# An adaLN block with sliding-window attention: V made per query group, an input load moved ahead, and packed matmul sums that choose their order

## The chip, the cores and the metric

The kernel runs on one core of a Trainium2 chip. The metric is the device time of one execution in microseconds (us), as the median of several runs. A core has a matmul engine (TensorE, PE), a vector engine (VectorE, DVE), an activation engine (ScalarE, ACT), a general engine (GpSimd, POOL) and a queue engine (SyncE, SP). They run in parallel, each in its own order, and wait for each other on semaphores. DMAs are issued from the queues of SP, ACT and POOL and share 16 DMA engines. The working memory SBUF has 128 rows, called partitions; matmuls write to PSUM, which has eight banks.

## What is computed

A transformer block over 2048 tokens of width 448, all in bf16, with six modulation rows made from a conditioning vector c. The attention has 16 heads of 28; each query sees 8 keys, at distances 0, 2, ..., 14 behind it.

```python
mod = (silu(c) @ w_mod).reshape(6, 448)            # sa, ca, ga, sb, cb, gb
h = layernorm(x) * (1 + ca) + sa
q, k, v = split(h @ wqkv)                          # 16 heads of 28
idx = pos[:, None] - 2 * arange(8)                 # keys of a query; masked where < 0
o = softmax(q . k[idx] * 28 ** -0.5) @ v[idx]
x = x + ga * (o @ wo)
h = layernorm(x) * (1 + cb) + sb
y = layernorm(h)                                   # the MLP has its own layernorm
x = x + gb * (gelu(y @ w1 + b1) @ w2 + b2)         # w1: 448 x 1792
```

## The kernel before

**Tokens.** The input is read so that even tokens make the first 1024 columns and odd tokens the second: with that order the dilated window of 8 becomes 8 neighbours. There are 16 blocks of 128 tokens, in four chunks of four blocks. Blocks 0 to 7 are the even tokens, 8 to 15 the odd ones.

**Front** (`front_ln`, `front_qk`). For each block VectorE takes statistics (L528, L529) and writes z, the normalized block (L551). For chunks 0 and 1 PE transposes z (L664) and VectorE and ACT write the modulated transpose hT (L679, L683); the factors come from PE matmuls on the first modulation load wm_st (L583). For chunks 2 and 3 the reciprocal root is taken on POOL (L546), SP issues one transposing DMA for each block (L688), and VectorE modulates in place (L692). Then Q and K are made, transposed, as four packed tasks for each group of blocks, and copied out by ACT (L732). V is made for two blocks of tokens at a time, tokens on partitions (pv, L609 and L615), and ACT copies it to vstage (L746). From there an ACT-queue DMA writes it to a DRAM buffer v_hbm (L750).

**Packed tasks** (`packed`). A width of 448 is 3.5 times 128. Two outputs are made together: three full matmuls of 128 rows each (`full`, L609) and one of 64 rows each (`half`, L615), the two of 64 rows in two halves of the array at once. Full and half are different array modes. Whether a task begins with full or with half is fixed by a turn counter of its kind (qk, v, w1), even or odd, so that two tasks of a kind in a row meet in the same mode.

**Attention** (`attention`). Queries are taken in 18 groups of 114, in 9 pairs b = 0 to 8. A group consists of two subgroups of 57 queries with 64 keys each. The logits of both subgroups of a group go to upper and lower partitions of a bank (lt, L829); ACT takes exponentials (et, L839), VectorE masks them (L847), PE makes denominators and outputs (pd L861, po L869), ACT inverts the denominators by logarithm and exponential (L882, L885), and VectorE multiplies (L895). The po matmuls need V in key rows: partitions 0 to 63 hold the keys of subgroup 0, and 64 to 127 those of subgroup 1, which begin 57 keys later. That is what the two SP-queue loads `vb<-v_hbm` of each pair (L815) bring.

**Behind it.** `out_proj` for each block: pw (L910), residual (L914), second layernorm, modulation (L925, L927), third layernorm to y, and a transposing DMA to yT (L936). `mlp` for each chunk: first layer p (L609, L615; seven packed tasks), gelu on ACT (L969), second layer (L982), residual (L990) and store. wo is scaled by ga (L776) and w2 by gb (L791) ahead of use. ga, sb, g2 and gb come from the later modulation: PE makes the rows from the loads wmod2 (L764), ACT evacuates them (L770) and writes them to DRAM (L772), and SP reads them back broadcast as mod_bc (L773).

**What sets the order.** Every instruction is a task with an engine, an assumed duration and buffers. `Planner.plan` tries 300 random perturbations of the priorities in a small timing model, keeps the cheapest plan, and `emit` writes each engine's instructions in that order. The seed fixes the draw. A task whose mode equals PE's current mode gets a bonus (SAME), a change of mode costs SWITCH in the model. ROOM holds the numbers of buffers. Bulk loads go on the POOL queue one after another (`bulk_loads`): wmod2 (4), wo (4), x of blocks 8 to 11, x of blocks 12 to 15, b2, w1 (4), w2 (4); each is released by a VectorE memset of one element (L385). The phases are: attention 0 to 4 and MLP 0, attention 5 and 6 and MLP 1, attention 7 and 8 and MLP 2 and 3.

Of the kernel before, what the change touches and what calls it, by code (L numbers as in the profile page):

```python
# [26 lines left out]
WQ, WK, WE = 57, 64, 58  # L27
SBQ, NSB, NBT = 2 * WQ, 18, 9
# [8 lines left out]
SEED, TURNS = 7, 300  # L37
QKE = ("AAAAAAAA", "AAAAAAAA")
# [6 lines left out]
FRONTS = (0, 1, 3)  # L45
LMM, DMM = 0.59, 1.0
FILL_UNTIL, FILL_SHARE = 12.0, 1.0
ROOM = {"S": 8, "et": 2, "den": 2, "zh": 6, "zb": 5, "T": 4, "hm": 4, "vb": 2, "vs": 2, "xp": 6}
DMA_RATE, TR_BYTES = 340e3, 400e3
SWITCH, SAME = 0.095, 1.0  # L50
SEM = 0.07
# [17 lines left out]
class Task:  # L69
    def __init__(self, n, eng, us, fn, bufs, rank_add, late, dense, port, mode):  # L70
        self.n, self.eng, self.us, self.fn, self.bufs = n, eng, us, fn, bufs
        self.name = f"{eng} {fn.__qualname__.split('.')[-1]}:{fn.__code__.co_firstlineno}"
        self.rank_add, self.late, self.dense, self.port = rank_add, late, dense, port
        self.mode_in, self.mode_out = mode if isinstance(mode, tuple) else (mode, mode)
        self.before, self.after = {}, []
        self.rank = 0.0
        self.fill = 0


class Planner:  # L80
# [68 lines left out]
    def forward(self):  # L149
# [13 lines left out]
        while len(order) < len(self.tasks):  # L163
            started = False
            for e in ("PE", "DVE", "ACT", "POOL", "SP", "BW"):
# [4 lines left out]
                for t in ready[e]:  # L170
                    if ready_at[t] > now or (shared and t.port):
                        continue
                    key = (-ready_at[t], -t.n) if e == 'BW' else (t.rank + (SAME if e == "PE" and t.mode_in == mode else 0.0), -t.n)
# [23 lines left out]
                if e == "PE" and t.mode_in != mode:  # L197
                    end += SWITCH
                    mode = t.mode_out
# [44 lines left out]
    def plan(self):  # L244
# [4 lines left out]
        for turn in range(TURNS):  # L249
# [4 lines left out]
            for again in range(3):  # L254
# [7 lines left out]
                if cost < best[2]:  # L262
                    best = ([(t, t.fill) for t in order], {b: b.slot for t in order for b in t.bufs}, cost)
                    starts = {t: t.start for t in order}
                    kept = used
# [7 lines left out]
    def emit(self):  # L273
        for t, fill in self.order:
            if fill:
                self.filler(fill)
            t.fn()
# [3 lines left out]
def kernel(  # L281
# [44 lines left out]
    v_hbm = hbm.tile([WT, DP], BF16, name="v_hbm")  # L326
# [28 lines left out]
    vstage = [cst.tile([128, 2, H, HP], BF16, name=f"vstage{i}") for i in range(ROOM["vs"])]  # L355
# [74 lines left out]
    def v_pads():  # L430
        z = warm_w[0:LEAD, :]
        o = v_hbm[0:LEAD, :]
        nc.sync.dma_start(out=bass.AP(o.tensor, o.offset, [[DP, LEAD], [(SL + SEP) * DP, 3], [1, DP]]),
                          in_=z.unsqueeze(1).to_broadcast([LEAD, 3, DP]))

    dma("SP", 0.5, v_pads, 3 * LEAD * DP * 2, ["v_pads"], reads=["warm_w"], order_after=chain["head"])
# [14 lines left out]
    def bulk_loads():  # L451
        for i in range(2):
            load_m(bulk, nc.gpsimd, lambda i=i: wmod2[i].t[:], (2 + 2 * i) * D, f"wmod2{i}", [wmod2[i]], True)
        wo_v = A_wo.rearrange("(ft r d) n -> r d ft n", r=4, d=DH)
# [3 lines left out]
        load_x(bulk, nc.gpsimd, 8, 12, True)  # L458
        load_x(bulk, nc.gpsimd, 12, 16, True)
# [49 lines left out]
    def consts():  # L509
        for vs in vstage:  # L510
            nc.gpsimd.memset(vs[:, :, :, DH:HP], 0.0)
# [89 lines left out]
    def packed(outs, w, x, turn):  # L601
# [3 lines left out]
        def full(last):  # L605
            for i in range(2):
                kts = (0, 3, 1 + i)
                for n, kt in enumerate(kts):
                    nc.tensor.matmul(outs[i].t[:], lhsT=w(i, kt, slice(0, 128)), rhs=x(i, kt, slice(0, 128)),  # L609
                                     start=(n == 0 and not last), stop=(n == 2 and last))  # L610

        def half(last):
            for i, kt, r0 in halves:
                rows = slice(r0, r0 + 64)
                nc.tensor.matmul(outs[i].t[:], lhsT=w(i, kt, rows), rhs=x(i, kt, rows),  # L615
                                 start=not last, stop=last, tile_position=(r0, 0))

        if turn % 2 == 0:
            full(False)
            half(True)  # L620
        else:
            half(False)
            full(True)

    def pack_mode(turn):
        return ("F", "64x128") if turn % 2 == 0 else ("64x128", "F")

    def pack_us(n):
        return 7 * (n / 2400 + 0.0025) + 0.008 + SWITCH

    turns = {"qk": 0, "v": 0, "w1": 0}
    h_of = {}

    def front_ln(bs):
        ch = bs[0] // 4
        early = ch <= 1
        if ch not in h_of:
            h_of[ch] = sb("T", [128, KT, 512], BF16, "hT")
# [12 lines left out]
        n, o = 128 * len(bs), (bs[0] % 4) * 128  # L651
# [35 lines left out]
        for b in bs:  # L687
            dma("SP", 1.25, lambda b=b: nc.sync.dma_start_transpose(out=hc.t[:, :, b % 4 * 128:b % 4 * 128 + 128], in_=zs[b].t[:]),  # L688
# [20 lines left out]
    def front_qk(bs, engs):  # L709
        n, c0, o = 128 * len(bs), tok_col(bs[0]), bs[0] % 4 * 128  # L710
        hc = h_of[bs[0] // 4]
        hk = [(hc, kt, b) for kt in range(KT) for b in bs]
        for mp in range(4):
            ms = (2 * mp, 2 * mp + 1)
            half = mp // 2
            pq = [ps_one([128, n], "pq") for _ in ms]
            turn = turns["qk"]
            turns["qk"] += 1

            def mm(mp=mp, half=half, pq=pq, turn=turn):  # L720
                packed(pq, lambda i, kt, rows: Wqk[rows, kt, half, (2 * mp + i) % 4 * 4:(2 * mp + i) % 4 * 4 + 4, :].rearrange("p r e -> p (r e)"),
                       lambda i, kt, rows: hc.t[rows, kt, o:o + n], turn)

            P.wrote(add("PE", pack_us(n), mm, mode=pack_mode(turn), reads=[f"W{half}{mp % 2}"] + hk, bufs=[hc] + pq), *pq)
            for i, m in enumerate(ms):
                dst = (qT if m < 4 else kT)[:, m % 4, c0:c0 + n]
                w = [f"{'q' if m < 4 else 'k'}{m % 4}_{b}" for b in bs]
                if engs[m] == "D":
                    add("DVE", 0.07 + n / 960, lambda dst=dst, p=pq[i]: nc.vector.tensor_copy(out=dst, in_=p.t[:]), bufs=[pq[i]],
                        writes=w)  # L730
                else:
                    add("ACT", 0.06 + n / 1200, lambda dst=dst, p=pq[i]: nc.scalar.copy(out=dst, in_=p.t[:]), bufs=[pq[i]],  # L732
                        writes=w)
        for b in bs[::2]:
            pv = [ps_one([128, D], "pv") for _ in range(2)]
            vs = Buf("vs", lambda k: vstage[k], "vs")
            turn = turns["v"]
            turns["v"] += 1

            def vmm(b=b, pv=pv, turn=turn):  # L740
                packed(pv, lambda i, kt, rows: hc.t[rows, kt, (b + i) % 4 * 128:(b + i) % 4 * 128 + 128],
                       lambda i, kt, rows: Wv[rows, kt, :], turn)

            P.wrote(add("PE", pack_us(D), vmm, mode=pack_mode(turn), reads=["wva", "wvb"] + hk, bufs=[hc] + pv), *pv)
            for i in range(2):
                add("ACT", 0.43, lambda i=i, pv=pv, vs=vs: nc.scalar.copy(  # L746
                    out=vs.t[:, i, :, 0:DH], in_=pv[i].t[:].rearrange("p (h d) -> p h d", h=H)),
                    bufs=[pv[i], vs], reads=["vpad"], writes=[(vs, i)])
            r0 = tok_col(b)
            dma("ACT", 0.5, lambda r0=r0, vs=vs: nc.scalar.dma_start(  # L750
# [322 lines left out]
```

## Time and profile before

| what | value |
|---|---|
| median of 11 runs | 184.95 us (180.74 to 186.73) |
| the profiled execution's own time | 184.91 us |
| its span, first to last instruction | 183.2 us |
| PE busy | 171.1 us (93%) |
| DVE, ACT, POOL busy | 113.2, 108.1, 58.4 us |
| DMA | 19.84 MB |
| mean granted clock of PE | 0.981 |

The page of a profile has the span cut into 40 slices, where a digit is the busy share of a slice in tenths, with a row for the PE clock that was granted. The chain of waits goes from the last instruction back to what released each step. Groups show line, engine, operation, output and inputs, count, busy time, mean duration in ns, and the idle time just before them. A DMA's time to landing is from issue to the signal that it has arrived. Times within the run are us from the start of the span.

### The profile page before, as it was taken

The numbers are of one execution on the slowest core, as the hardware profiler recorded it, in microseconds if no ns is written. First come the engines' busy times: TensorE is split into PE (matmuls) and PEld (weight loads), VectorE is DVE, ScalarE is ACT, GpSimd is POOL, SyncE is SP. The second block draws the span as 40 slices with busy tenths as digits, with TensorE's granted clock in tenths as the row PEclk, the third lists the DMA queues.
The fourth block names the chain that finished last, engine by engine and source line by source line (L and its number), as shares of the span: only waits on it lengthen the run. The fifth ranks groups of instructions, "written<-read, shape, count | busy, mean of one in ns | idle before, by whom it ended". The sixth has DMA issues, their size and how long they took to land.

```text
span 183.2 us, 5059 instructions
## 1 busy us (share of the span) xinstructions
PE 171.1 (93%) x2082; PEld 81.2 (44%) x2082; DVE 113.2 (62%) x333; ACT 108.1 (59%) x195; POOL 58.4 (32%) x99
## 2 busy tenths in 40 slices
PE   7799999987199999999999999999999999999993
PEld 2546564344023434533455534455543345433462
DVE  3476625985499999988553427998669972100121
ACT  2227988978324689797664993755893820177200
POOL 4056750264096561143122004436033443000000
PEclk9999999999659999999999999999999999999999
DMA  5988699759928967330311320004310024100011
GB/s 158 295 266 226 190 264 287 193 101 251 143 63 233 283 139 195 96 86 0 66 24 54 111 59 5 0 0 111 61 52 4 0 57 107 50 0 4 0 50 50
DMA packets 25245, 19.84 MB, mean 108 GB/s; under 512 B 14441, under 2 KB 23846, under 8 KB 25222
## 3 DMA queue, kind: packets, MB, share of 16 engines
q1 hardware_dynamic: 21372, 10.94, 24.2%
q0 software_dynamic: 1664, 6.48, 12.7%
q10 hardware_dynamic: 2186, 2.10, 4.5%
q8 instruction: 16, 0.26, 0.6%
q14 instruction: 7, 0.06, 0.1%
HBM read 12.41 MB, written 3.96 MB: 89 GB/s over the span
## 4 chain that ended last, share of the span: by engine, by line
PE 79%; DMA 12%; ACT 3%; POOL 1%; DVE 1%; issue 1%; SPq 0%; POOLq 0%; DVEq 0%
PE p L982 24%; PE p L609 21%; PE pq L609 10%; PE pw L910 6%; PE p L615 5%; DMA hT<-z 4%; PE pv L609 4%; DMA mod_bc<-mod_hbm 3%; DMA wm_st<-in_w_mod_dram 3%; PE pq L615 2%; PE po L869 2%; DMA mod_hbm<-mod_rows 2%; PE lt L829 2%; PE pwm L521 1%; ACT hT L683 1%
## 5 line engine op out<-in xcount | busy, mean ns | idle before, releaser
L969 ACT ACTIVATE hm<-p,b_col 128x512 bf16<-128x512 f32 x56 | 34.9, 685 | 26.3 <-PE p L609 19.4
L982 PE MATMUL p<-w_s,hm 128*128 128x448 bf16 (+1 forms) x238 | 44.5, 342 | 0.0
L609 PE MATMUL p<-yT,w_s 128*128 128x512 bf16 x168 | 39.3, 380 | 0.0
L940 POOL TENSOR_TENSOR x1p<-x_all,gbb_bc 128x448 f32<-128x448 bf16 x16 | 17.4, 1096 | 49.5 <-DVE x_all L914 31.4
L990 DVE TENSOR_TENSOR x_all<-p,x1p 128x448 bf16<-128x448 f32 (+1 forms) x17 | 10.1, 595 | 34.6 <-PE p L982 34.6
L546 POOL TENSOR_TENSOR rs_all<-tv_all,neg_half 128x1 f32<-128x1 f32 (+1 forms) x34 | 21.5, 649 | 29.5 <-DVE tv_all L543 23.5
L982 PEld LDWEIGHTS <-hm 128*128 128x128 bf16 x238 | 22.3, 98 | 18.9 <-issue 0.9
L609 PE MATMUL pq<-hT,Wqk 128*128 128x512 bf16 (+1 forms) x120 | 26.0, 363 | 4.2 <-DVE hT L692 4.2
L609 PEld LDWEIGHTS <-w_s 128*128 128x128 bf16 x168 | 15.1, 97 | 20.7 <-issue 4.6
L839 ACT ACTIVATE et<-lt 128x464 bf16<-128x464 f32 x36 | 17.4, 566 | 10.1 <-PE lt L829 9.9
L528 DVE BATCH_NORM_STATS2 st_all<-x_all 128x6 f32<-128x448 bf16 x32 | 18.7, 612 | 5.5 <-DMA x_all<-in_A_x_dram 5.4
L609 PEld LDWEIGHTS <-Wqk 128*128 128x128 bf16 x120 | 11.2, 103 | 16.3 <-issue 5.3
L732 ACT CAST qT<-pq 128x512 bf16<-128x512 f32 (+1 forms) x20 | 9.2, 511 | 12.0 <-PE pq L615 9.9
L551 DVE TENSOR_SCALAR z<-x_all,mv,rs_all 128x512 bf16<-128x512 bf16 (+1 forms) x32 | 11.9, 398 | 5.8 <-ACT rs_all L537 3.2
L910 PE MATMUL pw<-wo_s,oT 128*128 128x448 bf16 x64 | 14.0, 354 | 0.7 <-DVE oT L895 0.7
L914 DVE TENSOR_TENSOR x_all<-pw,x_all 128x448 bf16<-128x448 f32 x16 | 9.6, 614 | 5.7 <-PE pw L910 5.7
L847 DVE TENSOR_TENSOR et<-et,mask 128x928 bf16<-128x928 bf16 x18 | 11.2, 654 | 2.3 <-ACT et L839 2.3
L895 DVE TENSOR_TENSOR oT<-po,den 128x456 bf16<-128x456 f32 x18 | 10.5, 623 | 1.7 <-ACT den L885 1.7
L609 PE MATMUL pv<-Wv,hT 128*128 128x448 bf16 x48 | 10.4, 354 | 0.0
L882 ACT ACTIVATE den<-pd 128x464 f32<-128x464 f32 x18 | 9.1, 562 | 2.3 <-PE pd L861 1.7
L732 ACT CAST kT<-pq 128x512 bf16<-128x512 f32 (+1 forms) x20 | 9.0, 505 | 2.1 <-PE pq L615 2.1
L746 ACT CAST vstage<-pv 128x448 bf16<-128x448 f32 x16 | 8.0, 550 | 3.4 <-PE pv L615 1.9
(92 smaller groups left out, 182.9 us busy)
## 6 DMA issues: line engine op xcount, KB each, us to landing
w_s<-in_B_w_dram POOLq DMA_DIRECT2D x7, 448.0 KB, 4.9
vb<-v_hbm SPq DMA_DIRECT2D x18, 128.0 KB, 3.2
v_hbm<-vstage ACTq DMA_DIRECT2D x8, 256.0 KB, 3.6
wmod<-in_w_mod_dram POOLq DMA_DIRECT2D x4, 392.0 KB, 4.8
out_dram<-x_all SPq DMA_DIRECT2D x7, 224.0 KB, 2.2
wqk_st<-in_A_wqkv_dram SPq DMA_DIRECT2D x4, 226.0 KB, 6.2
x_all<-in_A_x_dram POOLq DMA_DIRECT2D x2, 448.0 KB, 6.1
wm_st<-in_w_mod_dram SPq DMA_DIRECT2D x2, 392.0 KB, 4.9
```

What stands on the lines that cost most here:

```text
L528: add("DVE", 0.53, lambda: nc.vector.bn_stats(out=st_all[:, sl, :], in_=src()), reads=key, writes=[f"st{sl}"])
L546: lambda: nc.gpsimd.tensor_tensor(out=rs_all[:, which, b0:b0 + n], in0=tv_all[:, which, b0:b0 + n], in1=neg_half[:, 0:n], op=ALU.pow),
L551: return add("DVE", us, lambda: nc.vector.tensor_scalar(out=dst(), in0=src(), scalar1=mv[:, b, 0:1], scalar2=rs_all[:, which, b:b + 1], op ...
L609: nc.tensor.matmul(outs[i].t[:], lhsT=w(i, kt, slice(0, 128)), rhs=x(i, kt, slice(0, 128)), start=(n == 0 and not last), stop=(n == 2 and ...
L615: nc.tensor.matmul(outs[i].t[:], lhsT=w(i, kt, rows), rhs=x(i, kt, rows), start=not last, stop=last, tile_position=(r0, 0))
L732: add("ACT", 0.06 + n / 1200, lambda dst=dst, p=pq[i]: nc.scalar.copy(out=dst, in_=p.t[:]), bufs=[pq[i]], writes=w)
L839: ex = add("ACT", 0.45, lambda r=r: nc.scalar.activation(out=et.t[:, r].rearrange("p n ft c -> p (n ft c)"), in_=lts[r].t[:].rearrange("p ...
L847: nc.vector.tensor_tensor(out=ev, in0=ev, in1=mask[:], op=ALU.mult)
L910: nc.tensor.matmul(pw.t[:], lhsT=oT[:, ft, c0:c0 + 128], rhs=wo_s[:, ft, :], start=(ft == 0), stop=(ft == 3))
L940: P.wrote(add("POOL", 1.05, lambda: nc.gpsimd.tensor_tensor(out=xp.t[:], in0=x_all[:, t, :], in1=gbb2_bc[:], op=ALU.add), reads=[f"x{t}", ...
L969: gl = add("ACT", 0.57, lambda f=f, p=p1[i]: nc.scalar.activation(out=hm_at(f), in_=p.t[:], func=ACT.Gelu_apprx_tanh, bias=b1_col[:, f:f + ...
L982: nc.tensor.matmul(p2.t[:], lhsT=hm_at(f)[:, bi * 128:(bi + 1) * 128], rhs=w2_s[:, f, c0:c1], start=(f == 0), stop=(f == FT - 1))
```

## The change

Four edits, and a new seed for the planner:

1. *V per query group.* `values(b)` makes V for one pair of groups directly in key rows: the stationary operand is a run of 128 columns of hT that begins at the group's first key, so the output's partitions are the 128 keys from there on. Partitions 0 to 63 of the copy (vkeys) are used by subgroup 0 in place; one SP-queue DMA from SBUF to SBUF moves partitions 57 to 120 to partitions 64 to 127 of vb for subgroup 1. v_hbm, its pads, the ACT-queue writes and the two loads of each pair go. There are 9 V tasks in place of 8.
2. *Edges.* A group's 128 keys can begin in the chunk before. hT gets 64 columns ahead of its 512 and 16 behind them; `h_edges` fills them by a VectorE copy from the chunk before or by POOL memsets.
3. *x ahead.* In `bulk_loads` the load of blocks 8 to 11 goes first, that of blocks 12 to 15 behind wmod2 and ahead of wo. FRONTS, which says after which attention pair each front is registered, goes from (0, 1, 3) to (0, 2, 3).
4. *Packed sums.* The turn counters go. A packed task has mode "flex": it begins with full if PE is in full mode at that place of the plan and with half otherwise, and the plan records which.

```diff
+HL, HTW = 64, 592
+VENG = "SP"
-SEED, TURNS = 7, 300
-QKE = ("AAAAAAAA", "AAAAAAAA")
+SEED, TURNS = 19, 300
-FRONTS = (0, 1, 3)
+FRONTS = (0, 2, 3)
-ROOM = {"S": 8, "et": 2, "den": 2, "zh": 6, "zb": 5, "T": 4, "hm": 4, "vb": 2, "vs": 2, "xp": 6}
+ROOM = {"S": 8, "et": 2, "den": 2, "zh": 6, "zb": 5, "T": 4, "hm": 4, "vb": 3, "vs": 2, "xp": 6}
+FLEX = ("F", "64x128")
...
                 end = now + t.us
-                if e == "PE" and t.mode_in != mode:
+                if e == "PE" and t.mode == "flex":
+                    t.closing = mode != "F"
+                    end += 0.0 if mode in FLEX else SWITCH
+                    mode = "F" if t.closing else "64x128"
+                elif e == "PE" and t.mode != mode:
                     end += SWITCH
-                    mode = t.mode_out
+                    mode = t.mode
...
     def bulk_loads():
+        load_x(bulk, nc.gpsimd, 8, 12, True)
         for i in range(2):
             load_m(bulk, nc.gpsimd, lambda i=i: wmod2[i].t[:], (2 + 2 * i) * D, f"wmod2{i}", [wmod2[i]], True)
+        load_x(bulk, nc.gpsimd, 12, 16, True)
         wo_v = A_wo.rearrange("(ft r d) n -> r d ft n", r=4, d=DH)
...
-        load_x(bulk, nc.gpsimd, 8, 12, True)
-        load_x(bulk, nc.gpsimd, 12, 16, True)
...
-        if turn % 2 == 0:
+        if closing:
+            half(False)
+            full(True)
+        else:
             full(False)
             half(True)
-        else:
-            half(False)
-            full(True)
...
-            h_of[ch] = sb("T", [128, KT, 512], BF16, "hT")
+            h_of[ch] = sb("T", [128, KT, HTW], BF16, "hT")
...
+    def h_edges(ch):
+        hc = h_of[ch]
+        if ch % 2 == 0:
+            add("POOL", 0.1, lambda: nc.gpsimd.memset(hc.t[:, :, HL - WIN:HL], 0.0), writes=[(hc, "lead")], bufs=[hc])
+            return
+        hp, b = h_of[ch - 1], 4 * ch - 1
+        add("DVE", 0.2, lambda: nc.vector.tensor_copy(out=hc.t[:, :, 0:HL], in_=hp.t[:, :, 512:512 + HL]),
+            reads=[(hp, kt, b) for kt in range(KT)], writes=[(hc, "lead")], bufs=[hp, hc], port=True)
+        add("POOL", 0.1, lambda: nc.gpsimd.memset(hc.t[:, :, HL + 512:HTW], 0.0), writes=[(hc, "tail")], bufs=[hc])
+
+    def values(b):
+        vk, vb = v_of[b] = Buf("vb", lambda k: vkeys[k], "vk"), sb("vs", [128, 2, H, HP], BF16, "vb")
+        pv = [ps_one([128, D], "pv") for _ in range(2)]
...
+        pair = (pv, lambda i, kt, rows: srcs[i][0].t[rows, kt, srcs[i][1]:srcs[i][1] + 128], lambda i, kt, rows: Wv[rows, kt, :])
+        P.wrote(add("PE", pack_us(D), lambda closing: packed([pair], closing), mode="flex", reads=["wva", "wvb"] + keys, bufs=hs + pv), *pv)
+        for i in range(2):
+            add("ACT", 0.43, lambda i=i: nc.scalar.copy(
+                out=vk.t[:, i, :, 0:DH], in_=pv[i].t[:].rearrange("p (h d) -> p h d", h=H)),
+                bufs=[pv[i], vk], reads=["vpad"], writes=[(vk, i)])
+        dma(VENG, 0.5, lambda: (nc.scalar if VENG == "ACT" else nc.sync).dma_start(out=vb.t[WK:2 * WK], in_=vk.t[WQ:WQ + WK]), 128 * DP * 2, [(vb, 1)],
+            reads=[(vk, 0), (vk, 1)], bufs=[vk, vb])
...
-                                             lhsT=vb.t[rows, n, ft * 4 + r, :], rhs=et.t[rows, r, n, ft, 0:WQ],
+                                             lhsT=(vb if j else vk).t[rows, n, ft * 4 + r, :], rhs=et.t[rows, r, n, ft, 0:WQ],
...
+    h_edges(0)
+    front_qk([2, 3])
+    values(0)
+    values(1)
...
-                front_qk(bs, QKE[1])
+                h_edges(fc)
+                front_qk(bs)
+                for v in ((2, 3), (4, 5), (6, 7, 8))[fc - 1]:
+                    values(v)
```

## The prediction

> **What bounds the kernel now.** I read the page's slices first, to see which engine is full and when.
>
> ```profile
> PE   7799999987199999999999999999999999999993
> DVE  3476625985499999988553427998669972100121
> PEclk9999999999659999999999999999999999999999
> ```
>
> A slice is 183.2 / 40 = 4.58 us. TensorE (PE) is busy nearly everywhere: 171.1 of 183.2 us. Only one place inside the run is empty: slices 8 to 10, about 36.6 to 50.4 us, ending in a "1". In the two slices after it (45.8 to 55 us) the granted clock falls to 0.6 and 0.5. From 50 us on PE never rests until the tail. So a gain must come from that hole, from the clock after it, or from PE work itself.
>
> Next, the chain of waits in order of time shows how the hole comes about. Columns: start, duration, what.
>
> ```profile
> 1.83 5.74 DMA wm_st<-in_w_mod_dram
> ...
> 26.88 3.44 DMA mod_hbm<-mod_rows
> ...
> 30.34 5.86 DMA mod_bc<-mod_hbm
> ...
> 40.48 7.67 DMA hT<-z
> ...
> 48.24 1.39 DVE hT L692 x4
> ...
> 49.68 2.74 PE pq L609 x6
> 52.42 0.54 PE pq L615 x2
> 52.96 1.96 PE pq L609 x6
> ...
> 58.72 1.40 PE pq L609 x6
> 60.12 0.32 PE pq L615 x2
> ...
> 70.10 2.70 PE pq L609 x12
> ```
>
> PE stops when its last attention matmuls end at 45.47 and starts at 49.68, when the third token chunk (blocks 8 to 11) has been transposed by DMA and modulated by VectorE (DVE). Its first eight matmuls then take 2.74 + 0.54 us, where the same shapes later take 1.40 + 0.32.
>
> The list of waits gives the hole's price, on PE and on DVE, which stands in the same wait (columns: waiting, awaited: total us, times, longest):
>
> ```profile
> DVE hT L692 <- DMA hT<-z: 4.6, 1, 4.6
> PE pq L609 <- DVE hT L692: 4.2, 1, 4.2
> SPq L815 <- PE po L869: 6.9, 2, 4.6
> ```
>
> Last, the DMA issues: number, size, median us to landing.
>
> ```profile
> vb<-v_hbm SPq DMA_DIRECT2D x18, 128.0 KB, 3.2
> v_hbm<-vstage ACTq DMA_DIRECT2D x8, 256.0 KB, 3.6
> wmod<-in_w_mod_dram POOLq DMA_DIRECT2D x4, 392.0 KB, 4.8
> x_all<-in_A_x_dram POOLq DMA_DIRECT2D x2, 448.0 KB, 6.1
> ```
>
> **x ahead of the later modulation.** Now the x load of blocks 8 to 11 is issued at 23.43 us, behind four wmod loads (1,568 KB) and four wo loads (392 KB), and VectorE's first statistics of it start at 29.40. Moved to the head of POOL's bulk loads it can go where the first wmod load goes now, at 11.29; with the 6.1 us of its own row it lands at 17.4. In before, 5.0 us pass from landing to the first transpose (34.39), and 13.8 from there to the landing of the last that PE waits for (48.15), SP's queue and a full DMA included; then 1.4 of modulation. That makes 17.4 + 5.0 + 13.8 + 1.4 = 37.6 us, against 45.5 when PE runs dry. There is 8 us of margin, so I take the hole as gone: **-4.2**. With it goes the low clock: (2.74 - 1.40) + (0.54 - 0.32) + (1.96 - 1.40) = **-2.1**.
>
> A rule speaks against the early load: the Trainium skill, "SBUF — State Buffer", section "SBUF: two separate sides", says that a DMA of GpSimd's queue can't write its descriptors while a two-port VectorE operation holds the shared port, and gives 3.1 us instead of 0.62. VectorE runs four Wqk copies up to 11.2 us and statistics after them. In this trace POOL's issues of such loads last 0.55 to 0.84 us, that at 11.29 itself 0.84. By the row nothing is lost; by the rule 2.5 us, and the chunk would be ready at 40.1, still before 45.5. The sum is the same, so I take the row.
>
> What the swap makes late: the wmod loads stand behind 448 KB (459 kB) more. At the 213 and 262 GB/s moved in 10-20 and 20-30 us that is 1.8 to 2.2 us. Everything behind mod_bc (36.2 us: scaled wo, gbb2, the first out-projection at 40.05) moves by about 2. The wo loads go behind 896 KB, some 4 us, and land near 31, before the modulation that they are multiplied with. Blocks 12 to 15 come about 1.5 us sooner (392 KB less ahead).
>
> Is MLP 0 in time? Its first matmul is at 76.96. Without the hole and the low clock PE has done all before it at 76.96 - 6.3 = 70.6, plus the added V task: some 72. The last of its four y tiles is written at 73.03 and its matmuls start 3.9 us later. Before that y, VectorE stands 4.64 us in the wait shown and does four w2 scalings (2.2 us, 69.51 to 71.74) that MLP 0's first layer doesn't need. So y can come at 68.4, or 66.2 with the scalings put behind it, and MLP 0 at 70.1 to 72.3, or 2 later if the late modulation passes through. Bounds: 0 to 2.3 us of new wait; I take **+0.5**, nearer the lower end since later tiles and attention can fill.
>
> **V per query group.** Today 8 V tasks (six full matmuls, two half ones); then 9, one per pair of query groups, because neighbouring groups' key rows overlap. PE: one more task at 1.24 + 0.29 from the chain's rows, **+1.5**. ACT: 18 evacuations for 16, 2 x 0.55 = +1.1, less eight DMA issues of 0.366 = -2.9. SP: 18 vb issues of 0.587 and one pad write of 0.34 go (10.9 us of its queue), 9 come (5.3). Bytes: 8 x 256 + 18 x 128 KB go, 9 x 128 KB come, about -3.2 of 19.84 MB, nearly all before 80 us, where the transposes land. No SBUF-to-SBUF copy is in the trace. From both sides: 1.5 us (the 56 KB store) to 6.0 (slowest vb load), nearest row the vb load, same size and same 64 partitions, 3.2. The lower half needs no DMA at all, and the trip of V is one transfer instead of two in series (3.6 + 3.2), so this is costed at 0 on the path: the exponentials and the mask of a group (4 x 0.566 + 2 x 0.654 = 3.6 us) run beside it. Without that cover a group would wait its 3.2. Each new copy waits on SP for two ACT evacuations and for an upper buffer that an earlier group's matmuls free; behind it queue the transposes, and for those VectorE and PE. That wait is there today (6.9 us, the third wait shown), with twice the DMAs.
>
> New helpers: two VectorE copies of 64 columns x 4 (the row of a 128x1024 copy says 0.42, so at most 0.8 in all) and a few POOL memsets (0.23 each). They lie in VectorE's 5.9 and POOL's 5.2 us idle of 20-30 us; without that cover, 1 us.
>
> The earlier V should also shorten PE's small gaps between 10 and 45 us (0.42 + 0.66 + 1.10 = 2.2 us by the ten-microsecond windows, the hole left out). From 0 to -2.2; a third of them wait for VectorE or ACT work on et and oT that starts sooner now: **-0.8**.
>
> **Sums that open or close by PE mode.** Switching between full and 64-row matmuls costs 2 x 1.40 - 2.70 = 0.10 us (six and twelve matmuls in the chain). Today the alternation is fixed, so a full-array task between two packed ones often costs two extra switches; in PE's timeline I count eight such returns (58.3, 86.8, 113.2, 133.5 ... 168.4). A task free to choose saves one each: 8 x 0.10 = **-0.8**. Bounds: 0, and 2.2 if all 22 of 119 mode changes that aren't forced went.
>
> **Sum** on the profiled span: 183.2 - 4.2 - 2.1 + 0.5 + 1.5 - 0.8 - 0.8 = 177.3. That execution's time is 184.91, 1.7 beyond its span, and at the median of the runs, 184.95. So 177.3 + 1.7 = **179.0 us**, -3.2%. All instructions are also re-planned from another seed, which changes the order everywhere; that is in the range, not in the sum.
>
> **Rivals.**
> 1. *The hole moves to MLP 0.* VectorE is 9.7 to 9.9 busy in each ten microseconds from 50 to 80, so y may not come sooner. With half of the 6.3 us recovered by y, the wait at MLP 0 is about 3 us: 179.0 + 3 - 0.5 = 181.5; with none, MLP 0 stays at 76.96 and the time is 184. What a wait costs here hangs on the clock: the row says that 4.2 us idle costs 2.1 more, half again, so 3 us would cost 4.5 (183.0). The Trainium skill, "TensorE: Matmul & The Clock Gate", section "Part 1: The HAM clock gate", says the clock is halved only after an idle window of about 3.4 us: then 3 us cost 3 (181.5). No gap between 0.74 and 4.2 us is in this trace to tell; I center this rival at 182.5. For it: VectorE's fullness. Against: the 4.64 + 2.2 us above.
> 2. *Slower: the late modulation sets MLP 0.* From mod_bc's landing (36.2) to MLP 0 it is 40.8 us. If that distance is rigid, 2.1 us later modulation puts MLP 0 at 79.1; PE idles over 4 us there and gets the low clock (+2.1): 183.2 + 2.1 + 2.1 - 0.5 (switches behind it) + 1.7 = 188.6. From about 2.2 us of delay it is over 2% slower. Against it: that distance holds VectorE's 4.64 us wait, which has another cause.
> 3. *The reorder doesn't reach the chip.* POOL's loads are released by tiny VectorE memsets in VectorE's order; if that for x waits behind statistics, x lands late, the hole stays: 184.9 + 1.5 - 0.8 - 0.8 = 184.8. Against: the first bulk load is released before 11.3 us today.
> 4. *More is recovered*: all small gaps and switches, no wait at MLP 0: 179.0 - 0.5 - 1.4 - 1.4 = 175.7.
>
> **How the numbers follow.** Forecast case 0.60 (176.5 to 181), case 4 0.10, rival 1 0.16, rival 3 0.06, rival 2 0.08. About 2% is what a measurement of this kernel tells from no change: 181.25 and 188.65. Faster: 0.60 + 0.10 + a quarter of rival 1 = 0.74; slower 0.08; within 0.18. The range runs from below case 4 to the upper end of rival 1: 175.0 to 184.0. The likeliest case's own range is 176.5 to 181.
>
> **What would show it.** Right: blocks 8 to 11 statistics near 18 to 20 us; no PE wait over 1 us between 20 and 70; clock 0.9 or more in every slice after the first; MLP 0 at 70 to 73; 9 V tasks, 18 evacuations; under 17 MB moved. Wrong: a low clock digit later on, PE waiting for yT, first out-projection later than 44 us, or po matmuls waiting for the new copy.

## The result, and the profile after

The changed kernel's median is 180.82 us (178.9 to 183.62, 12 runs), beside 184.49 us of the kernel before on the same chips (180.74 to 189.16, 47 runs). The medians differ by 2.0%. The ratio is 0.987, 95% interval [0.982, 0.992]: 1.3% off, where 3.2% was forecast. The profiled execution took 181.43 us, with a span of 179.7. Medians here are of all runs; ratios compare only each kernel's fast runs, within 1.5% of its fastest, and where these are too few no ratio is given.

First the slices of the page, as before.

```profile
PE   6799998867999999999999999999999999999992
DVE  2578957739779999997053538999999532000121
PEclk9999999995699999999999999999999999999999
```

A slice is 4.49 us now. The "987" and "1" in PE's row have become "8867": no slice is empty now, but PE is six to eight tenths busy from 27 to 45 us. The low digits of the clock, 5 and 6, are still there. The hole is shallower and wider, and the clock is not restored.

Then the chain of waits in order of time (start, duration, what).

```profile
22.04 5.99 DMA x_all<-in_A_x_dram
...
28.60 1.13 DVE st_all L527 x2
29.73 0.64 DVE z L550 x2
...
32.09 6.55 DMA hT<-z
...
39.00 1.09 DVE wo_s L785 x2
...
42.35 1.68 PE pw L909 x4
...
44.74 1.61 PE pw L909 x4
46.35 2.24 PE pq L608 x6
...
75.21 1.29 PE p L608 x6
```

The path to the third chunk's Q and K (pq at 46.35, before at 49.68) begins with a load of x again, though that chunk's x came early. It is the *other* load, of blocks 12 to 15, which lands at 28.03. The list of waits and VectorE's timeline say why (waits: waiting, awaited: total us, times, longest; timeline: start, us, instruction, in brackets the idle time before it).

```profile
DVE st_all L527 <- DMA x_all<-in_A_x_dram: 6.4, 3, 3.1
DVE z L550 <- DMA hT<-z: 2.9, 1, 2.9
PEld L909 <- DVE wo_s L785: 1.6, 1, 1.6
PE pw L909 <- ACT et L838: 1.5, 1, 1.5
PE pw L909 <- DVE oT L894: 1.2, 1, 1.2
```

```profile
28.05 1.68 DVE L527 BATCH_NORM_STATS2 st_all<-x_all 128x6 f32<-128x448 bf16 x3 [3.09 <-DMA x_all<-in_A_x_dram]
29.65 0.72 DVE L550 TENSOR_SCALAR z<-x_all,mv,rs_all 128x512 bf16<-128x512 bf16 x2
38.67 0.41 DVE L550 TENSOR_SCALAR z<-x_all,mv,rs_all 128x512 bf16<-128x512 bf16 x1 [2.94 <-DMA hT<-z]
```

The statistics at 28.05 are those of blocks 12 to 15. VectorE works in order, so the z of blocks 8 to 11 (29.65) stand behind an instruction that waits 3.09 us for another chunk's data. Their own statistics were done by 23.3, and POOL's reciprocal root for them, behind two wo issues, began at 26.13. The first transpose then starts at 30.08, only 4.3 us sooner than before. The fourth and last of this chunk's transposes is issued at 34.69, and the last signal of it comes at 41.62 (the landing at 38.64 in the chain is that of the second). The modulation follows from 42.21 to 44.68. A second wait of the same kind, 2.94 us at 38.67, for a z of blocks 12 to 15, keeps VectorE from scaling wo (39.00) and from the next oT. PE's first two out-projections wait for these, 1.52 us at 40.21 and 1.21 at 42.35 (the list puts the first of them down to et, but the weight load PEld of that matmul waits for wo_s). For the chunk itself PE doesn't wait any more: pq follows an out-projection without a gap.

Last, the new copy and the transposes (issues: number, size, median us to landing).

```profile
vb<-vkeys SPq DMA_DIRECT2D x9, 128.0 KB, 3.9
hT<-z SPq DMA_TRANSPOSE x8, 6.6
```

The two profiles differ by 3.5 us of span: PE's idle time fell by 2.4 us (12.1 to 9.7) and its busy time by 1.1 (171.1 to 170.0). MLP 0 begins at 75.04 instead of 76.96, so 1.9 us of the 3.5 lie ahead of it. The other 1.6 lie behind it, 104.7 us for 106.2, where PE has no gap in either kernel: the changed one has one out-projection fewer left there (four matmuls, some 0.9 us) and ten mode changes fewer.

### The profile page after: what moved, and what is told of

Its sections match the earlier page's. It is cut to its first block, busy times and chain, and to the rows that moved or that the text cites. A ratio compares the mean times of both kernels' runs of the same rounds, so it can differ in the third digit from the quotient of the medians.

```text
span 179.7 us, 5054 instructions
## 1 busy us (share of the span) xinstructions
PE 170.0 (95%) x2090; PEld 82.2 (46%) x2090; DVE 114.3 (64%) x335; ACT 108.3 (60%) x197; POOL 60.6 (34%) x104
## 2 busy tenths in 40 slices
DMA packets 21165, 16.54 MB, mean 92 GB/s; under 512 B 14161, under 2 KB 19190, under 8 KB 21142
## 3 DMA queue, kind: packets, MB, share of 16 engines
HBM read 10.05 MB, written 1.84 MB: 66 GB/s over the span
## 4 chain that ended last, share of the span: by engine, by line
PE 71%; DVE 10%; DMA 10%; ACT 4%; issue 2%; SPq 1%; DVEq 0%
PE p L979 24%; PE p L608 21%; PE pw L909 7%; PE pq L608 5%; PE p L615 4%; DMA hT<-z 4%; DMA x_all<-in_A_x_dram 3%; DMA wm_st<-in_w_mod_dram 3%; PE pv L608 3%; DVE z L550 2%; DVE st_all L527 2%; PE lt L828 2%; DVE oT L894 2%; PE po L868 2%; PE pwm L520 1%
## 5 line engine op out<-in xcount | busy, mean ns | idle before, releaser
L545 POOL TENSOR_TENSOR rs_all<-tv_all,neg_half 128x1 f32<-128x1 f32 (+1 forms) x34 | 22.5, 676 | 30.9 <-DVE tv_all L542 25.2
L939 POOL TENSOR_TENSOR x1p<-x_all,gbb_bc 128x448 f32<-128x448 bf16 x16 | 18.3, 1148 | 36.8 <-DVE x_all L913 17.8
L608 PE MATMUL pq<-hT,Wqk 128*128 128x512 bf16 (+1 forms) x120 | 24.5, 347 | 0.0
L909 PE MATMUL pw<-wo_s,oT 128*128 128x448 bf16 x64 | 15.6, 381 | 2.9 <-ACT et L838 1.5
L550 DVE TENSOR_SCALAR z<-x_all,mv,rs_all 128x512 bf16<-128x512 bf16 (+1 forms) x32 | 14.2, 459 | 5.5 <-DMA hT<-z 2.9
L608 PE MATMUL pv<-Wv,hT 128*128 128x448 bf16 x54 | 11.6, 353 | 0.0
L724 ACT CAST kT<-pq 128x512 bf16<-128x512 f32 (+1 forms) x20 | 9.5, 516 | 2.6 <-PE pq L615 2.0
L909 PEld LDWEIGHTS <-oT 128*128 128x128 bf16 x64 | 5.9, 102 | 9.6 <-DVE oT L894 2.1
L757 ACT CAST vkeys<-pv 128x448 bf16<-128x448 f32 x18 | 8.9, 549 | 2.3 <-PE pv L615 1.6
```

Of the source, the lines that this page charges most:

```text
L545: lambda: nc.gpsimd.tensor_tensor(out=rs_all[:, which, b0:b0 + n], in0=tv_all[:, which, b0:b0 + n], in1=neg_half[:, 0:n], op=ALU.pow),
L550: return add("DVE", us, lambda: nc.vector.tensor_scalar(out=dst(), in0=src(), scalar1=mv[:, b, 0:1], scalar2=rs_all[:, which, b:b + 1], op ...
L724: add("ACT", 0.06 + n / 1200, lambda dst=dst, p=p: nc.scalar.copy(out=dst, in_=p.t[:]), bufs=[p], writes=w)
L909: nc.tensor.matmul(pw.t[:], lhsT=oT[:, ft, c0:c0 + 128], rhs=wo_s[:, ft, :], start=(ft == 0), stop=(ft == 3))
L939: P.wrote(add("POOL", 1.05, lambda: nc.gpsimd.tensor_tensor(out=xp.t[:], in0=x_all[:, t, :], in1=gbb2_bc[:], op=ALU.add), reads=[f"x{t}", ...
```

## The experiments

Theory A, after reading this: the third chunk is late because of VectorE's order, and a part of the gain is lost there. Theory B: the chunk isn't what sets the time; from 40 to 62 us VectorE is the bound (the chain holds many of its pieces there), so filling PE's hole or restoring its clock brings little, which is rival 1. Theory C: the plan's new draw, which the forecast kept out of the sum, is as large as the edits. "Fixed plan" below means the planned order of the kernel named, with only the tasks named moved or altered; `shift(tasks, anchor)` puts tasks behind the anchor in that order.

**Controls.** Each kernel once more, unchanged.

> The kernel before once more, for a second profile of it. If the hole before 49.7 us and the low clock after it belong to the kernel, both come again: one PE wait of about 4 us for hT, some 6.6 us of halved clock, span 181 to 184 us. If they belonged to that one execution, the wait is under 2 us and the clock full.

> The changed kernel again, unchanged, beside the others of this set on the same chip: ratio to before 0.98 to 0.99, first out-projection near 40, MLP 0 near 75 us.

The kernel before: 183.25 us, span 181.5, with the same wait of PE for hT (4.1 us), but with the clock low for 3.4 us instead of 6.8. Of the 1.7 us by which this span is shorter, 1.1 are there at pq already (48.55 for 49.68), and as much at the first out-projection, ahead of the low clock; 0.6 come between pq and MLP 0 (26.68 us for 27.28), where the low clock lies. So about half of the 3.5 us between the first two profiles is no more than two executions of one kernel differ by. The kernel after: 0.989 [0.983, 0.995], 181.41 us, MLP 0 at 75.59. The result stands.

**z of blocks 8 to 11 first** (A), fixed plan of after: the statistics of blocks 12 to 15 and what follows from them go behind the last z of blocks 8 to 11.

```diff
     P.plan()
+    shift([428, 426, 432, 430, 427, 431, 433, 429, 434], 334)
     P.emit()
```

> The changed kernel with its plan held fixed, but on VectorE the statistics of blocks 12 to 15 (which wait for the x load) put behind the last z of blocks 8 to 11. Theory A (VectorE's order keeps the third chunk): z at 27.3 instead of 29.7 to 32.6 us, the chunk's first QK matmuls 2 to 3 us earlier than 46.1, PE idle between 30 and 50 us falls from 3.9 to about 2, time 1.5 to 3 us under the changed kernel (ratio to before about 0.975). Rival (the transposes' landing in a full DMA sets it, 6.6 us each): z comes earlier, hT doesn't, time within 0.5 us of the changed kernel (0.987).

Measured: 0.971 [0.962, 0.980], 180.62 us, profiled span 177.4. VectorE's and PE's timelines:

```profile
26.34 0.74 DVE L550 TENSOR_SCALAR z<-x_all,mv,rs_all 128x512 bf16<-128x512 bf16 x2 [2.27 <-POOL rs_all L545]
42.91 2.55 PE L608 MATMUL pq<-hT,Wqk 128*128 128x512 bf16 x6
```

z is 3.3 us sooner, pq 3.2 us sooner (46.14 in after's timeline), MLP 0 at 72.75, 2.3 us sooner, as is the end. So A holds as far as the cause goes: nine instructions moved on one queue bring the chunk forward. How much time that is worth is less sure. In this execution the clock was low for 3.4 us instead of 6.8, which is a part of the 2.3. The interval lies below the control's, but it rests on two of six runs; the median of all six is 2.0% under the kernel before's, as the changed kernel's own was at first, where the control's is 1.8%. What z now waits for is POOL's reciprocal root, which stands behind two wo issues there.

**Root ahead of wo as well**, fixed plan: `shift([93, 94, 95, 96], 332)` is added.

> The changed kernel with its plan held fixed and two moves: on VectorE the statistics of blocks 12 to 15 behind the last z of blocks 8 to 11 (as before), and on POOL the reciprocal root of blocks 8 to 11 ahead of the first two wo loads, whose issues held it for 1.2 us. Theory (VectorE's waits between 20 and 50 us set when MLP 0 starts): MLP 0 at 71.5 to 73 us, time 2 to 3.5 us under the changed kernel, 0.3 to 1.2 under the version with the first move alone. Rival (the wo scaling or the transposes' landing sets it next): no more than the first move's 2.3 us.

0.976 [0.968, 0.984], 179.59 us, beside the control's 181.41 on the same chip: again below the changed kernel, and by the ratio no better than z first alone. Its profile, of an execution of 182.03 us and so not of a usual one, has VectorE waiting 2.94 and 1.62 us for transposes and MLP 0 at 75.66.

**PE's gaps filled** (B against the clock), fixed plan: seven and six full matmuls on zeros ahead of the first two out-projections; they open the bank anew and leave the sums as they are.

```diff
         def mm():
+            for k in range({0: 7, 1: 6}.get(fills.index(t) if t in fills else -1, 0)):
+                nc.tensor.matmul(pw.t[:], lhsT=warm_w[:, 0:128], rhs=warm_w[:, 0:D], start=True, stop=True)
             for ft in range(4):
```

> The changed kernel with its plan held fixed, but 7 and 6 extra full matmuls on zeros ahead of the first two out-projections, written to their banks before the real sums start there; they run in PE's waits at 38.7 and 41.1 us. Theory B (the clock is halved for want of array work, not for one long wait): the clock stays 1.0 in 40 to 50 us and the time falls by the 2.5 us that the slow matmuls cost now, ratio to before about 0.974. Rival (the halved clock has another cause, or the time behind it is set by VectorE): clock or time stay, ratio 0.987, or up to 0.3 us more for matmuls that run into the real ones.

(What is called Theory B there is that the clock falls for want of array work; its rival is the B of this section.) 0.998 [0.994, 1.001], 182.86 us: neither 0.974 nor 0.987, but about 1% above the control. The clock row and the same six matmuls:

```profile
PEclk9879999999999999999999999999999999999999
```

```profile
45.97 1.46 PE L608 MATMUL pq<-hT,Wqk 128*128 128x512 bf16 x6
```

The clock is full from 14 us on, and six matmuls take 1.46 us instead of after's 2.45. Yet from the first out-projection (40.98) to MLP 0 (75.83) it is 34.85 us; in after it is 75.04 - 40.21 = 34.83. I took this for B: a low clock that lies under VectorE's work and costs nothing. The traces don't bear that out. After's chain, shown above, goes through the slow matmuls (1.68, 1.61, 2.24), and in the fill run the two oT that follow them begin 9.93 us after the first out-projection (50.91), where it was 11.86 (52.07). What was gained went into a wait of PE with no named cause, in the middle of a tile. It lies on this run's chain (start, duration, what):

```profile
48.07 0.51 PE po L868 x59
48.58 1.81 issue
50.39 0.21 PE po L868 x5
```

VectorE then stands 1.84 us, until 56.35, for a PE out-projection behind it. The changed kernel has no such wait; more on them below. So this run doesn't tell what the low clock costs: by the two oT 1.9 us up to there, by MLP 0 nothing.

**x ahead alone**, in the kernel before, planned anew from seed 7; FRONTS stays as it was.

```diff
     def bulk_loads():
+        load_x(bulk, nc.gpsimd, 8, 12, True)
         for i in range(2):
...
+        load_x(bulk, nc.gpsimd, 12, 16, True)
         wo_v = A_wo.rearrange("(ft r d) n -> r d ft n", r=4, d=DH)
...
-        load_x(bulk, nc.gpsimd, 8, 12, True)
-        load_x(bulk, nc.gpsimd, 12, 16, True)
```

> The kernel before with the x loads of blocks 8 to 15 moved ahead as in the change and nothing else, re-planned from its own seed 7. As predicted, the hole of 4 us and its clock go: ratio about 0.965. By what the changed kernel showed (z behind statistics, landing in a full DMA): 0.98 to 1.0. If the draw of the plan outweighs the edit, anything from 0.97 to 1.03.

1.001 [0.997, 1.004]. The hole at 45 to 50 us is gone (the wait for hT is 1.62 us, at 39.6), and this stands in PE's timeline instead:

```profile
75.03 0.93 PE L910 MATMUL pw<-wo_s,oT 128*128 128x448 bf16 x4 [2.05 <-DVE tv_all L543]
```

PE is busy for 7.69 of the ten microseconds from 70 to 80. MLP 0 begins at 76.22 (before: 76.96), when the transpose of its last y tile has landed; the chain leads to that tile through VectorE, which is busy for 9.93 of those ten microseconds. The hole didn't close, it moved to where VectorE's work is next needed. This is rival 1 on the chip, for x alone.

**x loads put back**, in the kernel after, planned anew from seed 19 (the reverse of the last diff).

> The changed kernel with the x loads of blocks 8 to 15 back behind wmod and wo, re-planned from seed 19: V in key rows and packed sums stay. If the early x load is worth what was predicted, the hole of about 4 us before the third chunk's QK matmuls is back and the time 1 to 4 us above the changed kernel (ratio 0.99 to 1.01). Rival: VectorE sets MLP 0 either way and the hole is covered, ratio within 0.005 of the changed kernel; the modulation then comes 1 to 2 us sooner and may even make it faster.

0.996 [0.991, 1.000], 183.6 us, MLP 0 at 77.07. Against the control's 0.989 the early x is worth 0.6% here, but the two intervals overlap, and the plan differs too.

**Free order of the packed sums alone**, fixed plan of before: every packed task begins in the mode PE is in, 119 mode changes become 106.

```diff
             if fill:
                 self.filler(fill)
+            if t.eng == "PE":
+                if t.mode_in != t.mode_out:
+                    self.pick[0] = 0 if mode == "F" else 1
+                    mode = "F" if self.pick[0] else "64x128"
+                else:
+                    mode = t.mode_in
             t.fn()
```

> The kernel before with its plan held fixed, but each packed task begins in the mode that the task ahead of it left; nothing else of the change. The mode changes in PE's order fall from 119 to 106. At the 0.10 us of the prediction that is 1.3 us, ratio 0.993, if PE is the bound wherever they lie; rival: those that lie ahead of the hole at 45 us are swallowed by it, some 1 us remains (0.995) or nothing (1.0) if a mode change costs nothing when the next weights are loaded behind it.

1.005 [0.993, 1.017]. Thirteen changes at 0.10 us would be 0.7%; none of it is seen in the time. The interval reaches down to it, so a small gain isn't excluded. In its one profile a wait for yT, 1.33 us at 134.02, which the kernel before doesn't have, is larger than the whole gain would be.

**w1 held back**, fixed plan of after: three w1 loads are issued behind the modulation of blocks 8 to 11, so that the transposes have less company.

```diff
+    shift([104, 105, 107, 108, 106, 110, 111, 109], 348)
```

> The changed kernel with its plan held fixed, but the three w1 loads that go out at 34 to 42 us (448 KB each) held back behind the modulation of blocks 8 to 11. Theory C (the transposes of z land late, 6.6 us, because those loads fill the DMA): landing falls to 3 to 4.5 us, VectorE's 2.9 us wait for hT goes, MLP 0 starts 1.5 to 3 us sooner than 75, ratio to before 0.97 to 0.98. Rival (the transposes fill the DMA by themselves, eight of them in ten us): landing stays above 5.5 us, ratio 0.985 to 0.99.

(Its Theory C is one of the transposes, not that of the draw.) 0.987 [0.981, 0.994], as the control. Transposes land in 5.1 us instead of 6.6, but VectorE still waits 2.62 and 1.06 us for them, and MLP 0 is at 75.62.

**All together**, fixed plan: z first, root first, w1 late, and the last two z of blocks 12 to 15 behind that modulation (`shift([438, 437, 444, 442], 348)`).

> The changed kernel with its plan held fixed and every move at once: statistics of blocks 12 to 15 behind the z of blocks 8 to 11, the reciprocal root ahead of the wo loads, the last two z and transposes of blocks 12 to 15 behind the modulation of blocks 8 to 11 (so that wo's scaling doesn't stand behind a z that waits for a transpose to land), and the w1 loads held back. If VectorE's waits between 20 and 50 us set MLP 0: first out-projection at 37 to 38.5 us, MLP 0 at 70 to 72, ratio 0.96 to 0.97. Rival (beyond the first move the time is set by VectorE's work, not its waits): no better than the first move alone, 0.971 to 0.976.

0.985 [0.979, 0.991], 180.35 us: no better than z first alone (by the medians both are 2.0% under the kernel before). Here pq is at 41.73 and the clock is full from 14 us on, but what was deferred comes back:

```profile
52.03 0.42 DVE L688 TENSOR_SCALAR hT<-hT,mod_col 128x512 bf16<-128x512 bf16 x1 [2.60 <-DMA hT<-z]
```

PE then waits 1.18, 1.16 and 1.05 us between 54 and 61, and MLP 0 is at 73.60.

**The draw** (C). Both kernels planned from each other's seed:

```diff
-SEED, TURNS = 19, 300
+SEED, TURNS = 7, 300
```

> The changed kernel re-planned from the seed of before (7 for 19); everything else of the change stays. If the change's edits make the gain, 0.98 to 0.99 again; if the draw of the plan does, anything from 0.97 to 1.02, with PE's waits and VectorE's at other places. Both theories of this study expect that the place of the x statistics in VectorE's order differs.

> The kernel before, nothing of the change but the planner's new seed (19 for 7). The changed kernel lost 3.5% when its seed went to 7. If the draw alone can move the time by some per cent, this is away from 1.0 by over 1%; if the edits made the difference, within 0.5% of 1.0.

After from seed 7: 1.024 [1.012, 1.036]. Before from seed 19: 189.01 us beside 183.96, 2.7% more. After from seed 7 stops here (PE's timeline, and the DMA issues from 30 to 57 us):

```profile
56.11 0.24 PE L868 MATMUL po<-et,vb 64*32 64x57 bf16 x4 [6.11 <-DMA vb<-vkeys]
```

```profile
vb<-vkeys SPq DMA_DIRECT2D x2, 128.0 KB, 16.6
hT<-z SPq DMA_TRANSPOSE x5, 9.6
w_s<-in_B_w_dram POOLq DMA_DIRECT2D x5, 448.0 KB, 12.6
```

The copy of V was issued at 39.47, behind four transposes (33.76 to 39.3) on the same queue, beside five weight loads of 448 KB (four of w1, one of w2), and landed 16.6 us later. VectorE waits 9.19 us for a transpose there. Three more pairs, both kernels from the same seed:

> The changed kernel planned from seed 3, beside the kernel before planned from seed 3. If the 1.3% belongs to the edits, the changed one is 1 to 3% below its partner in every pair. If the draw decides, the pair's difference can have either sign and reaches 2 to 4%, and this run lies anywhere from 0.97 to 1.04 of the shown kernel before.

> The kernel before planned from seed 3. By the edits: 1 to 3% above its partner. By the draw: between 0.99 and 1.04 of the shown kernel before; above 1 more often than below, if the shown seed was a good draw.

> The changed kernel planned from seed 11; the same two expectations as for seed 3. If the wait of VectorE for chunk 3's transposes or of PE for the new V copy stands in its trace with more than 4 us, the draw has queued them behind each other on SP, and the time is over 1.01.

> The kernel before planned from seed 11; by the edits 1 to 3% above its partner, by the draw either side of it, between 0.99 and 1.04 of the shown kernel before.

> The changed kernel planned from seed 23. By the edits, 1 to 3% below its partner; by the draw, either side of it. After the pairs of seeds 3 and 11, I expect it level with its partner or up to 3% above, 1.00 to 1.03 of the shown kernel before.

> The kernel before planned from seed 23: between 0.99 and 1.03 of the shown kernel before.

| seed | before: median, profiled span | after: median, profiled span | PE waits over 1 us without a named cause, before / after |
|---|---|---|---|
| 7 | 184.49, 183.2 | 188.85, 187.5 | 0 / 2.1 |
| 3 | 184.33, 183.1 | 189.07, 185.8 | 0 / 6.1 |
| 11 | 184.36, 183.2 | 189.18, 188.0 | 2.6 / 9.6 |
| 23 | 186.10, 186.8 | 187.55, 190.2 | 3.7 / 8.6 |
| 19 | 189.01, 187.8 | 180.82, 179.7 | 0 / 0 |

Ratios to the shown kernel before: at seed 3 before 1.002 [0.997, 1.007]; at seed 11 after 1.023 [1.004, 1.042], before 1.014 [1.006, 1.022]; at seed 23 before 1.006 [1.001, 1.011]. After at seeds 3 and 23 has only four runs, from 184.33 to 193.78 and 183.49 to 191.9, and no ratio. In four of five pairs the changed kernel is the slower one, by 0.8 to 2.6% in the medians; only at seed 19 does it lead, by 4.3%. C holds, and more strongly than I thought: the shown gain belongs to these edits together with this draw, not to the edits in any plan. Why the draw matters so much is another question, and the last column bears on it.

That column was not foreseen. In the new pairs PE stops in the middle of a tile and the profile names nothing that it waits for. Seed 23 after, PE's timeline, and the DMA queues in the quarter microsecond from 44.70 (queue: packets, MB, time of these packets as a share of 16 engines in that stretch):

```profile
50.77 0.62 PE L828 MATMUL lt<-qT,kT 28*64 28x58 bf16 x44 [5.30 <-issue]
```

```profile
q8 instruction: 1, 0.02, 112.1%
```

That one packet is of the queue that the profile calls instruction, which I read as code. It took 1.121 x 16 x 0.25 = 4.5 us, from 44.9 to 49.4; PE goes on 1.4 us later. In after's own trace such packets take 0.9 to 1.5 us. In all runs there are 13 waits of PE of over 1 us with no named cause, all between 37 and 60 us, and in each a packet of this queue had ended 1.3 to 1.6 us before PE went on. Seed 11 after: ended 56.0, PE on at 57.27, after 8.50 us. Seed 11 before: 43.2 and 44.66. So these waits fit late code; no run changed the code's load alone, so that is read, not tested.

How much of the draw's effect that is can be estimated from the chains. Of these waits, 2.1, 4.8, 9.6 and 6.4 us lie on the chain of the kernel after at seeds 7, 3, 11 and 23, and 2.6 us on that of the kernel before at seed 11. Taken off the spans, with nothing else to take their place, that leaves 185.4, 181.0, 178.4 and 183.8 us for after, and 183.2, 183.1, 180.6 and 186.8 for before: the changed kernel would lead in three of these four. So the sign in these pairs may come from where such waits fall, more than from the edits. Each span is of one execution, and no run shows this.

## Why the prediction was wrong

Direction right, size wrong: -1.3% for -3.2%. The time, 180.82, is inside the range and inside the likeliest case's. By PE's account of the two profiles:

| | predicted | measured |
|---|---|---|
| PE idle: hole -4.2, small gaps -0.8, new wait +0.5 | -4.5 | -2.4 |
| PE busy: clock -2.1, ninth V task +1.5, switches -0.8 | -1.4 | -1.1 |
| span | -5.9 | -3.5 |

**The step that failed** is "There is 8 us of margin, so I take the hole as gone: -4.2". The sum behind it was 17.4 + 5.0 + 13.8 + 1.4 = 37.6; in after it is 18.0 + 12.1 + 11.5 + 3.1 = 44.7. The term that was mis-sized is the second, the 5.0 us from x's landing to the first transpose, taken over from the trace before: it became 12.1 (18.03 to 30.08). x was issued at 13.92, not 11.29, since the mask's set-up stands ahead of it on POOL. Then z waited for the root on POOL, and on VectorE behind statistics of blocks whose x landed at 28.03. That load in turn was issued only at 22.04, after POOL had waited 2.12 us for the VectorE memset of one element that releases it: the mechanism of rival 3, on the other x load. The forecast asked when x would land, and did not ask who stands ahead of z. The z-first run shows it: z 3.3 us sooner and MLP 0 2.3 us sooner in its trace. And PE still waits 2.7 us at 40.21 and 42.35, for wo and oT behind VectorE's next wait.

**"With it goes the low clock: -2.1"** failed with it. The low clock stayed: pw 1.68 and 1.61 where 0.86 is usual, pq 2.24 for 1.40, about 2.5 us of PE time, and these pieces are on the chain. What its end would have been worth stays open, since the fill run got a new wait on its chain. So **"MLP 0 at 70.1 to 72.3"** was wrong (75.04): neither of the two savings came in full. The wait for y that rival 1 put there isn't what sets it in the changed kernel. The last of the four y tiles is written by 70.2 (before: 73.4), and PE runs without a gap from 62.5 us to MLP 0. Rival 1's mechanism shows in the x-alone run, where the last y is written at 72.5 and its transpose sets MLP 0's start. Part of the agreement is luck: of the 3.5 us measured, 1.6 lie behind MLP 0, for which the forecast had 0.5, "switches behind it".

**The rule on the clock**, as rival 1 weighed it (the Trainium skill, "TensorE: Matmul & The Clock Gate", section "Part 1: The HAM clock gate": halved after an idle window of about 3.4 us), does not carry here as an "only", which is the prediction's word: the clock fell at about 41.3 us with no gap over 1.52 us, among attention matmuls that use a part of the array. In the kernel before it fell at about 47.2, 1.8 us after PE's last matmul (45.47). With the fill run's full matmuls in these gaps it stayed at full speed there.

**The new draw** was "in the range, not in the sum". It moved the kernel before by 2.7% (seed 19) and the kernel after by 4.4% (188.85 for 180.82), more than the whole forecast of 3.2%. That the shown pair came out faster at all is therefore luck in part.

**Right:** POOL's issue of the early x lasted 0.93 us, near the row and not the rule of the Trainium skill ("SBUF — State Buffer", section "SBUF: two separate sides"), which made 2.5 us more; nine V tasks and 18 evacuations; 16.54 MB, under 17; the first out-projection at 40.21, so that late modulation cost nothing seen (rival 2 did not come); the copy of V at 3.9 us for an estimate of 3.2, with no matmul waiting for it. That last holds for this order only: at seed 7 the same copy cost 6.1 us, the "without that cover" case, at twice its price. **Switches:** 17 fewer, for eight counted, 1.7 us by the same 0.10; when done alone nothing of it is seen in the time. Then clock (+0.4), V task and switches would give PE +0.2 busy, and it is -1.1: 1.3 us of that I can't assign. The two profiles of the kernel before differ by as much (171.1 and 169.5).

**Open:** how much of the gain each edit has in a given plan. x alone gives 1.001 in one plan and 0.6% in another, both planned anew. What the low clock costs, and whether late code makes the unnamed waits, is open too.

## What to carry to other kernels

Before you price a hole or a low clock on one engine, ask which engine sets the stage behind it. A fill that restores the clock without changing the order can answer that, if you then read its own chain: here it came with a new wait as long as the gain. Data that comes early is only used early if nothing on the consumer's in-order queue waits for later data ahead of it, so follow the whole queue, not only the transfer. Where a planner draws the order, compare edits inside a fixed plan and over several seeds, and look in each trace for waits that no edit made; one pair of draws can turn the sign.

## What the chip showed that was not expected

- The clock was halved 1.8 us after PE's last matmul in the kernel before, and in the kernel after with no gap over 1.52 us, among matmuls on parts of the array; see above.
- Code arrives by DMA, and it seems that it can be late: PE waits of 1.1 to 8.5 us ended 1.3 to 1.6 us after a packet of the instruction queue did, and one such packet took 4.5 us, where those of the kernel after take 0.9 to 1.5, while weight loads and transposes filled the DMA. The Trainium skill, "Runtime: NRT & Kernel Launch", section "Instruction fetch mechanics", has the next block fetched while the current one runs and the cost mostly hidden. In the shown kernels before and after no such wait is over 1 us; nine of the experiments have one or two.
- A transposing DMA's median time to landing went from 4.5 to 8.5 us from kernel to kernel; a 128 KB copy inside SBUF took 3.9 us, and 16.6 behind transposes and beside weight loads.
